# Local attention, a dense expert layer and a soft expert layer on one core: token groups of six tiles as the outermost loop, with later attention placed between the experts

## The chip, the core and the metric

The kernel runs on one core of one Trainium2 chip. Its time is the device time of one execution, in microseconds (us); lower is better. TensorE (PE, with its weight loads as PEld), VectorE (DVE), ScalarE (ACT), GpSimd (POOL) and SyncE (SP) each work through a queue of their own in a fixed order and wait for one another by semaphores. SP's work here is only to issue transfers.

## What is computed

```python
# 4 batches, 8 heads, 576 positions, head size 64; 2304 tokens of 512 values
scores = q @ k.T / sqrt(64) - slope[head] * |i - j|     # kept where 0 <= i - j < 128
x = softmax(scores) @ v                                  # tokens x 512
p = domain_probs / domain_probs.sum(-1)
x = sum over e of p[:, e] * (relu(x @ w1[e]) @ w2[e])    # 4 experts, 512 -> 1024 -> 512, every token
logits = x @ phi                                         # 32 slots, 4 for each of 8 experts
slots = softmax over tokens(logits).T @ x
slots[expert] = relu(slots[expert] @ m1[expert]) @ m2[expert]
out = softmax over slots(logits) @ slots
```

## The kernel before

There are 18 token tiles of 128 tokens. Nearly every product is made in fp16 with each operand split into a high and a low half, so that one product is three matmuls (high x high, high x low, low x high). Each split is one ACT copy and one DVE or POOL subtraction.

**Attention** runs in 72 steps, one for each tile and pair of heads, written in the loop over `n` from line 521. A step makes scores (`qk`, L364 and L369), masks and exponentiates them (L380 on DVE, L385 on ACT), splits them (L390, L391) and has them transposed by a DMA transpose that SP issues (L327, tile `eT`); three steps later the product with V follows (L411). For each tile SP also issues three loads (L304) and transposes of q, k and the result (`qT`, `kT`, `xT`). So SP issues about seven transposes a tile.

**Expert 0 of the dense layer** is laid into the attention steps: a list `pend` of pieces (L206 is the first layer, L234 the second) is worked off with a budget of about 2.8 us of matmuls a step. Tiles 0 and 1 are made in float32 (L273, L283).

**Experts 1 and 2 and half of 3** come after the attention, in units of one quarter of an expert's hidden width by six tiles (`unit_l1`, `unit_l2`). A unit's first layer replaces eight block products by seven (a Strassen-Winograd scheme with sums of x blocks, made once a group in `xsum_jobs`, L598 and L602, and sums of weight blocks, made once a quarter in `w7_jobs`, L641 and L646). It is 42 matmuls of 384 columns (L657); its second layer is 36 matmuls of 512 columns (L732). The units go expert quarter outermost, then the three groups of six tiles, so each weight quarter is loaded, split and summed once and serves three units. `l2_add` (L244) adds each unit's second layer to the accumulator in SBUF, six additions a unit.

**The other half of expert 3** is made in the plain form (L206, L234), with the soft layer's steps (`x2_tile`, `x2_log`, `x2_l`, `x2_d`) between its pieces. At last the soft layer's experts (`hp`, L1063; `so_ps`, L1081) read 64 weight blocks of 512 KB, which `pre` loads ahead (L826) into as many buffers as are free; a used buffer is filled again by `refill`. Then the outputs are made (L1094).

The order in which instructions stand on each engine is not that of the code: a scheduler decides it when the program is built, so the change can move instructions far.

Of the kernel before, what the change touches and what calls it, by code (L numbers as in the profile page):

```python
# [20 lines left out]
def kernel(  # L21
# [38 lines left out]
    slab = ctx.enter_context(tc.tile_pool(name="slab", bufs=23))  # L60
# [13 lines left out]
    def sl12(shape, dt, name):  # L74
        return slab.tile(shape, dt, tag="x12", name=nm(name), bufs=3)
# [65 lines left out]
    W = {}  # L141
    stg = {}

    def load_w(e, qd, part="ab"):
        if "a" in part:
            t = stg[e, qd, 0] = sl([P, KC, 256], F32, "stg")
            if e == 0:
# [7 lines left out]
        if "b" in part:  # L155
            t = stg[e, qd, 1] = sl([P, 2, 512], F32, "stg")
            if e == 0:
# [4 lines left out]

    def split_w(e, qd, j):
        m = j // 2
        if j % 2 == 0:
            W[e, qd, m] = sl([P, 2, 1024], F16, "w")
        a, b = (j % 2) * 512, (j % 2 + 1) * 512
        src, dst = stg[e, qd, m].rearrange("p k f -> p (k f)"), W[e, qd, m]
        nc.scalar.activation(out=dst[:, 0, a:b], in_=src[:, a:b], func=AF.Copy, scale=WS)
        nc.vector.scalar_tensor_tensor(out=dst[:, 1, a:b], in0=src[:, a:b], scalar=WS,  # L170
                                       in1=dst[:, 0, a:b], op0=ALU.mult, op1=ALU.subtract)
# [29 lines left out]
    def l1_piece(e, t0, n, fc, key):  # L201
# [7 lines left out]
        if e == 0:  # L209
            kk = (key, fc // 4)  # L210
            if kk not in hh:
                hh[kk] = sl([P, 4, 2, 256], F16, "h")
            ht = hh[kk][:, fc % 4, :, 0:n]
        else:
            kk = (key, fc // 2)
            if kk not in hh:
                hh[kk] = h3[h3n[0] % 2].rearrange("p (a b c) -> p a b c", a=2, b=2)
                h3n[0] += 1
            ht = hh[kk][:, fc % 2, :, 0:n]
# [5 lines left out]
    h3n = [0]  # L225

    def l2_mm(e, t, o, fcs, key, lo, hi):
# [3 lines left out]
        for fc in fcs[lo:hi]:  # L231
            ht = hh[key, fc // 4][:, fc % 4] if e == 0 else hh[key, fc // 2][:, fc % 2]
# [31 lines left out]
    def moe32_pieces(t):  # L264
        def l1(f0):
            if f0 == 0:
                h32[t] = sl([P, FC, P], F32, "h32")
# [31 lines left out]
    def ld(i, which="qkv"):  # L299
        for nme in which:  # L300
            src = {"q": q, "k": k, "v": v}[nme]
            t = at([P, H, D], F32, nme + "r")
# [69 lines left out]
    def soft(i, hp, st):  # L372
# [20 lines left out]
        eTt = at([P, 8, P], F16, "eT", 6)  # L393
# [4 lines left out]
    def pv(i, hp):  # L398
        if hp % 2 == 0:
            xps[i, hp // 2] = ps1.tile([P, 512], F32, tag=f"X{hp // 2}", name=nm("x"))[:, 0:4 * (D + 1)].rearrange(  # L400
# [76 lines left out]
    for qd in range(4):  # L477
        load_w(0, qd, part="b")
# [652 lines left out]
```

## Time and profile before

| | |
|---|---|
| median of 3 runs | 933.04 us (932.43 to 934.72) |
| profiled execution: span from first to last instruction | 933.0 us |
| mean granted TensorE clock | 0.984 |
| busy: PE, DVE, ACT, POOL | 878.7, 567.9, 362.0, 176.2 us |
| moved by DMA | 102.35 MB |

The profiled execution's own time is its span, 933.0 us, and the median of the runs is the same within 0.1 us, so a sum made against the span is made against the runs too. A matmul's record reaches past the point where the next one starts, so a PE shown as busy may still be slowed; the pace at which equal matmuls follow one another is the better measure of its work. Times below count from the first instruction.

### The profile page before, as it was taken

The page shows a single profiled execution, that of the slowest core. Times are in us where ns is not written, and L with a number is a line of the kernel's source. Part 1 is how long each engine was busy: PE and PEld are TensorE (multiplying, and loading weights), DVE is VectorE, ACT ScalarE, POOL GpSimd, SP SyncE. Part 2 cuts the span into 40 slices and gives each one's busy share as a digit, 9 for nine tenths or more (in the row PEclk, how much of TensorE's full clock was granted, in tenths as well). Part 3 has the DMA queues.
Part 4 walks back from the last instruction along what each step waited for, and adds up shares of the span by engine and source line. Part 5 has one row for each costly group of instructions (what it writes and reads, how often), then busy time and mean ns, then how long its engine had stood idle before and what let it go on. Part 6 is the DMA issues. An engine that isn't in the chain of part 4 may idle for free.

```text
span 933.0 us, 16170 instructions
## 1 busy us (share of the span) xinstructions
PE 878.7 (94%) x6426; PEld 517.2 (55%) x6426; DVE 567.9 (61%) x1271; ACT 362.0 (39%) x768; POOL 176.2 (19%) x173
## 2 busy tenths in 40 slices
PE   5897888898999999999999999999999999999797
PEld 4675665677675655555555555555555445564532
DVE  6775664654545997656575666666666554556612
ACT  5876665564652344323132323232333201223412
POOL 4565564554440000000000000000000005310000
PEclk9999999999999999999999999999999999999799
DMA  9889999997855110000101010101001008983796
GB/s 262 170 151 178 194 190 180 176 163 123 136 92 125 46 46 24 23 23 23 46 1 46 1 46 1 46 14 32 23 23 46 1 0 304 227 214 127 246 392 230
DMA packets 222028, 102.35 MB, mean 110 GB/s; under 512 B 187216, under 2 KB 201584, under 8 KB 221952
## 3 DMA queue, kind: packets, MB, share of 16 engines
q1 hardware_dynamic: 212320, 78.14, 39.4%
q10 hardware_dynamic: 6800, 13.11, 4.1%
q0 software_dynamic: 2832, 10.07, 3.0%
q8 instruction: 50, 0.82, 0.4%
q14 instruction: 26, 0.21, 0.1%
HBM read 64.59 MB, written 4.72 MB: 74 GB/s over the span
## 4 chain that ended last, share of the span: by engine, by line
PE 59%; issue 3%; DVE 2%; DMA 2%; POOL 1%; SPq 1%; ACT 0%; DVEq 0%; POOLq 0%; ACTq 0%
PE l L732 22%; PE A L657 12%; PE C L657 6%; PE l L206 4%; PE l L234 4%; PE B L657 3%; PE hp L1063 2%; PE so_ps L1081 2%; DMA m<-in_moe_w_dram 1%; PE fp L1094 1%; SPq L883 1%; DVE st L598 1%; POOL m L826 1%; PE lpb L892 0%; DMA xtc<-xsc 0%
## 5 line engine op out<-in xcount | busy, mean ns | idle before, releaser
L732 PE MATMUL l<-w,h 128*128 128x512 f16 x1080 | 252.8, 379 | 0.0
L244 DVE SCALAR_TENSOR_TENSOR acc<-l,pr,acc 128x512 f32<-128x512 f32 x216 | 161.6, 750 | 128.2 <-PE l L732 105.0
L657 PEld LDWEIGHTS <-w 128*128 128x128 f16 x1260 | 123.2, 98 | 95.3 <-issue 1.4
L732 PEld LDWEIGHTS <-h 128*128 128x128 f16 x1080 | 105.7, 98 | 115.2
L206 PE MATMUL l<-xT,w 128*128 128x256 f16 (+2 forms) x1152 | 150.5, 283 | 15.8 <-DVE h L221 10.9
L234 PE MATMUL l<-w,h 128*128 128x512 f16 x600 | 143.0, 379 | 0.7 <-DVE acc L244 0.7
L206 PEld LDWEIGHTS <-w 128*128 128x128 f16 x1152 | 105.9, 100 | 51.3 <-issue 17.4
L681 ACT ACTIVATE ct<-A 128x384 f32<-128x384 f32 x90 | 43.4, 487 | 205.5 <-PE A L657 205.5
L826 POOL DMA_DIRECT2D m<-in_moe_w_dram x19 | 13.7, 722 | 487.9 <-DVE h L677 424.5
L391 POOL TENSOR_TENSOR e<-e,e 128x512 f16<-128x512 f32 (+1 forms) x72 | 81.2, 1131 | 90.5 <-ACT e L390 60.8
L234 PEld LDWEIGHTS <-h 128*128 128x128 f16 x600 | 56.4, 98 | 56.7 <-issue 1.9
L220 ACT ACTIVATE h<-l 128x256 f16<-128x256 f32 (+2 forms) x96 | 36.4, 385 | 110.5 <-PE l L206 75.1
L385 ACT ACTIVATE e<-e,nmx 128x256 f32<-128x256 f32 (+1 forms) x144 | 63.4, 485 | 34.9 <-DVE nmx L380 34.7
L221 DVE SCALAR_TENSOR_TENSOR h<-l,h 128x256 f16<-128x256 f32 (+2 forms) x96 | 41.0, 432 | 54.7 <-ACT h L220 54.4
L657 PE MATMUL C<-xs,w 128*128 128x384 f16 x360 | 71.9, 326 | 0.0
L657 PE MATMUL A<-xs,w 128*128 128x384 f16 x360 | 69.6, 326 | 0.0
L657 PE MATMUL A<-xT,w 128*128 128x384 f16 x360 | 67.3, 326 | 1.0 <-issue 1.0
L380 DVE CUSTOM_DVE_ANT_0 e<-s,bias 128x256 f32<-128x256 f32 (+1 forms) x144 | 52.6, 404 | 14.4 <-PE s L369 12.7
L676 ACT ACTIVATE h<-ct 128x384 f16<-128x384 f32 x90 | 43.8, 515 | 44.6 <-PE l L732 29.2
L411 PE MATMUL x<-vv,eT 128*128 128x65 f16 (+1 forms) x816 | 42.9, 196 | 11.7 <-DMA eT<-e 9.2
L411 PEld LDWEIGHTS <-eT 128*128 128x128 f16 x816 | 36.6, 100 | 21.4 <-DMA eT<-e 12.2
L677 DVE SCALAR_TENSOR_TENSOR h<-ct,h 128x384 f16<-128x384 f32 x90 | 47.6, 553 | 1.2 <-ACT h L676 1.2
(185 smaller groups left out, 984.9 us busy)
## 6 DMA issues: line engine op xcount, KB each, us to landing
m<-in_moe_w_dram ACTq DMA_DIRECT2D x25, 512.0 KB, 6.0
stg<-in_moe_w_dram SPq DMA_DIRECT2D x20, 512.0 KB, 4.8
m<-in_moe_w_dram SPq DMA_DIRECT2D x20, 512.0 KB, 10.0
m<-in_moe_w_dram POOLq DMA_DIRECT2D x19, 512.0 KB, 12.5
stg<-in_moe_w_dram SPq DMA_DIRECT2D x24, 256.0 KB, 3.2
out_dram<-ots SPq DMA_DIRECT2D x18, 256.0 KB, 3.1
qr<-in_q_dram SPq DMA_DIRECT2D x16, 256.0 KB, 3.8
kr<-in_k_dram SPq DMA_DIRECT2D x16, 256.0 KB, 4.0
```

The source lines that it names most:

```text
L206: nc.tensor.matmul(pt, lhsT=w1_ap(e, fc, wa, kc), rhs=x_ap(t0, n, xa, kc), start=first_mm, stop=(kc == KC - 1 and wa == 1))
L234: nc.tensor.matmul(pt, lhsT=ht[:, ha, o:o + P], rhs=w2_ap(e, fc, wa), start=(fc == fcs[0] and ha == 0 and wa == 0), stop=(fc == fcs[-1] an ...
L244: nc.vector.scalar_tensor_tensor(out=a, in0=pt, scalar=p, in1=a, op0=ALU.mult, op1=ALU.add)
L380: mx = nc.vector.tensor_tensor_reduce(out=et[:, hl, c0:], in0=st[:, hl, c0:], in1=bias[:, h, c0:], op0=ALU.add, op1=ALU.min, scale=-0.125, ...
L385: nc.scalar.activation(out=et[:, hl, c0:], in_=et[:, hl, c0:], func=AF.Exp, scale=-1.0, bias=nmx[i][:, h:h + 1])
L391: nc.gpsimd.tensor_tensor(out=e2[:, :, 1], in0=et[:, :, c0:], in1=e2[:, :, 0], op=ALU.subtract)
L411: nc.tensor.matmul(o[:, 0:w], lhsT=t[:, (hl * 2 + ea) * nk + kb - kb0], rhs=vvs[i - 1 + kb][:, h, va, 0:w], start=(kb == kb0 and ea == 0 a ...
L657: nc.tensor.matmul(o, lhsT=wq_[:, blk, wa, kc], rhs=xf(xa, kc), start=(first and kc == 0 and wa == 0 and xa == 0), stop=(kc == 1 and wa == 1),
L676: nc.scalar.activation(out=o[:, 0], in_=src, func=AF.Relu)
L677: nc.vector.scalar_tensor_tensor(out=o[:, 1], in0=src, scalar=0.0, in1=o[:, 0], op0=ALU.max, op1=ALU.subtract)
L681: nc.scalar.activation(out=dst, in_=src, func=AF.Copy)
L732: nc.tensor.matmul(pt, lhsT=u["h"][:, z, ha, par, i * P:(i + 1) * P], rhs=w2_ap(e, 2 * qd + z, wa), start=(z == 0 and ha == 0 and wa == 0) ...
```

## The change

**Loops.** Token groups of six tiles (`sg`) become the outermost loop: `QU` lists 44 units, first group 0 with experts 1, 2, 3, then group 1 with 1, 2, 3, 0, then group 2 with 0 to 3. Only group 0 with expert 0 stays in the plain form, in the attention steps of the opening (`groups0` ends at tile 5). All else is made of seven products.

**Attention.** The opening runs only until group 0's expert 0 has been queued, about step 30. The other steps are spread over the units of groups 0 and 1 by `steps_to`, with goals `S_A` and `S_B`.

**Weights.** A quarter's split and summed operands are made once (`fresh`) and stored in DRAM (`keep`, 0.92 MB and 0.52 MB); 28 later units read them back (`again`), all on SP's queue.

**Second layer.** `half_l2` sums two quarters in PSUM before one addition, so three additions a unit on average instead of six.

**Buffers.** `slab` goes from 23 to 13 buffers; weights, sums and h tiles have pools of their own; the sums of x have one buffer instead of three; the matmul accumulators `A` and `B` of a unit share the two `L1` banks and `C` has one bank; raw q, k and v share four buffers, `eT` has five instead of six.

**Soft layer.** `x2_tile` and its followers of tiles 0 to 11 stand in the units of group 2. Of the 64 weight blocks 36 are loaded ahead (15 issued by POOL, the rest by SP) and 28 by `refill`; before it was 44 and 20, issued by POOL, ACT and SP.

```diff
-    slab = ctx.enter_context(tc.tile_pool(name="slab", bufs=23))
+    slab = ctx.enter_context(tc.tile_pool(name="slab", bufs=13))
+    sub = ctx.enter_context(tc.tile_pool(name="sums", bufs=1))
+    dram = ctx.enter_context(tc.tile_pool(name="dram", bufs=1, space=bass.MemoryType.DRAM))
...
+    def s12(shape, dt, name):
+        return sub.tile(shape, dt, tag="S12", name=nm(name), bufs=1)
+    def w7b(shape, dt, name):
+        return sub.tile(shape, dt, tag="w7", name=nm(name), bufs=2)
+    def h6(shape, dt, name):
+        return sub.tile(shape, dt, tag="h6", name=nm(name), bufs=5)
...
-        eTt = at([P, 8, P], F16, "eT", 6)
+        eTt = at([P, 8, P], F16, "eT", 5)
...
-    for z in [1, 1, 1, 1, 2, 2, 2, 2, 2, 2, 2]:
...
+    groups0 = [[0], [1], [2], [3], [4, 5]]
...
+    while avail:
+        n = nstep[0]
+        nstep[0] += 1
+        att_step(n, lambda: front(n))
+    def steps_to(n):
+        while nstep[0] <= min(n, NLAST):
+            att_step(nstep[0])
+            nstep[0] += 1
...
+    def keep(key, t, shape):
+        d = dW[key] = dram.tile(shape, F16, name=nm("dw"))
+        nc.sync.dma_start(out=d, in_=t)
...
+        def again():
+            W7[e, qd] = w7b(S7, F16, "w7")
+            nc.sync.dma_start(out=W7[e, qd], in_=dW["a", e, qd])
...
         def p1():
-            u["A"] = ps.tile([P, 512], F32, tag=f"S{n % 2}", name=nm("A"), bufs=1)[:, 0:N]
+            u["A"] = ps.tile([P, 512], F32, tag="L1", name=nm("A"))[:, 0:N]
...
-            u["C"] = ps1.tile([P, 512], F32, tag=f"X{n % 2}", name=nm("C"))[:, 0:N]
+            u["C"] = ps1.tile([P, 512], F32, tag="X1", name=nm("C"))[:, 0:N]
...
+    def half_l2(e, qds, sg, us, init, order):
...
+                                     start=(y == 0 and z == 0 and ha == 0 and wa == 0),
+                                     stop=(y == 1 and z == 1 and ha == 1))
+            if y == 1:
+                l2_add(e, t, l2p.pop((e, qds[0], t)), init)
...
+    QU = [(0, e, qd) for e in (1, 2, 3) for qd in range(4)]
+    QU += [(1, e, qd) for e in (1, 2, 3, 0) for qd in range(4)]
+    QU += [(2, e, qd) for e in range(4) for qd in range(4)]
...
+    def unit_jobs(x):
+        return (raw_at(x + 1, "b") + raw_at(x + 2, "a") + w2_jobs(*QU[x][1:], fresh[x]) + w7_at(x + 1))
...
+    S_A = [nstep[0] + (4 * 2 * TS + 4 - nstep[0]) * (x + 1) / 10.5 for x in range(12)]
+    S_B = [S_A[-1] + (NLAST + 1 - S_A[-1]) * (x + 1) / 14.0 for x in range(16)]
...
-    slb = ctx.enter_context(tc.tile_pool(name="slb", bufs=17))
+    slb = ctx.enter_context(tc.tile_pool(name="slb", bufs=14, reuse_waits="tile"))
...
-    pre(17, "slb")
+    pre(8, "slb")
+    pre(1, "x12")
+    for x in range(28, NU):
...
+        unit(x, sj)
+    dq[0] = nc.sync
+    pre(1, "x12")
+    pre(1, "S12")
+    pre(2, "w7")
```

**How the order changes: DVE, around attention steps 33 to 36.** Before, DVE's queue there holds attention (L380 is the masked score, L420 to L422 the normalization) and the low half of the plain first layer (L221).

```order
274 L420 TENSOR_SCALAR r_2116<-x_2028 128x4
275 L421 RECIPROCAL r_2116<-r_2116 128x4
276 L422 TENSOR_TENSOR x_2115<-x_2028,r_2116 128x256
277 L221 SCALAR_TENSOR_TENSOR h_1841<-l_307_1874,h_1841 128x256
278 L380 ISA e_2159,nmx_2050<-s_2150,bias_90 128x256
```

Now the sums of group 0's x blocks (L618 and L622, which were L598 and L602; `st` and `xs` are their tiles) stand among the scores of the following group (L392, which was L380).

```order
287 L618 TENSOR_TENSOR st_1923<-st_1923,st_1922 128x768
288 L618 TENSOR_TENSOR st_1922<-st_1922 128x768
289 L433 RECIPROCAL r_2291<-r_2291 128x4
290 L434 TENSOR_TENSOR x_1806<-x_1890,r_2137 128x256
291 L622 TENSOR_TENSOR xs_1921<-st_1923,xs_1921 128x768
292 L234 SCALAR_TENSOR_TENSOR h_1842<-l_303_1875,h_1842 128x256
293 L392 ISA e_2564,nmx_2563<-s_2558,bias_95 128x128
```

Before, no sum of x blocks and no split of summed weights (L646) stood ahead of the last score. Now group 0's sums and the first weight quarters' share DVE with attention steps 28 to 46, which the scheduler has drawn forward into the end of the opening and the first two units.

**How the order changes: SP, in the middle of the attention.** Before, SP's queue holds only transposes and loads of q, k and v.

```order
76 L327 DMA_TRANSPOSE eT_1739<-e_281_1736 128x8x128
77 L327 DMA_TRANSPOSE xT_652<-xs_1741 128x8x128
78 L327 DMA_TRANSPOSE kT_1923<-ks_1824 128x8x128
79 L304 DMA vr_2169<-in_v_dram 128x8x64
80 L327 DMA_TRANSPOSE eT_1777<-e_288_1774 128x8x128
```

Now the stores of weight operands (L655, `dw` is the DRAM tile) and their readings back (L665 and L689) stand among them, here in the first units of group 1.

```order
180 L339 DMA_TRANSPOSE eT_3905<-e_613_3902 128x8x128
181 L689 DMA w_4946<-dw_2618 128x2048
182 L655 DMA dw_4150<-w_640_4081 128x3584
183 L316 DMA raw_4675<-in_q_dram 128x8x64
184 L339 DMA_TRANSPOSE eT_4045<-e_635_4042 128x8x128
185 L339 DMA_TRANSPOSE qT_4338<-qs_4234 128x8x128
```

A store's condition is that its operand is made, a reading's that its buffer is free, and the transposes behind them now come after these in the queue.

## Rows read from the trace of the kernel before

**Rows 1.** The page, busy time of each engine.
```profile
PE 878.7 (94%) x6426; PEld 517.2 (55%) x6426; DVE 567.9 (61%) x1271; ACT 362.0 (39%) x768; POOL 176.2 (19%) x173
```

**Rows 2.** Windows: length, busy us of each engine (instructions), granted clock, DMA share, GB/s.
```profile
0.00:105.00 105.00, 82.14 (x940) 64.35 (x941) 70.69 (x239) 71.67 (x157) 58.48 (x63) 0.98 0.97 191
105.00:173.00 68.00, 57.89 (x627) 42.91 (x625) 37.99 (x140) 41.95 (x96) 35.32 (x32) 0.95 1.08 185
173.00:325.00 152.00, 143.12 (x1373) 101.67 (x1371) 92.20 (x254) 76.09 (x160) 54.86 (x47) 0.98 0.67 121
325.00:800.00 475.00, 475.00 (x2529) 247.37 (x2528) 305.95 (x516) 134.45 (x279) 18.19 (x23) 1.00 0.13 44
```

**Rows 3.** Chain of waits: start us, us, what.
```profile
311.16 1.31 PE l L206 x12
...
402.16 2.59 PE l L732 x12
...
411.24 1.95 PE A L657 x12
```

**Rows 4.** Waits of PE: us in total, times, longest.
```profile
PE l L206 <- DVE h L221: 10.9, 8, 3.3
PE x L411 <- DMA eT<-e: 9.2, 11, 1.9
```

**Rows 5.** Timeline of PE, first score products of attention steps 28 and 46.
```profile
105.19 0.22 PE L364 MATMUL s<-kT,qT 128*128 128x128 f16 x1
...
172.81 0.22 PE L364 MATMUL s<-kT,qT 128*128 128x128 f16 x1
```

**Rows 6.** Groups of DVE instructions by form: busy us, mean ns of one.
```profile
L244 DVE SCALAR_TENSOR_TENSOR acc<-l,pr,acc 128x512 f32<-128x512 f32 x216 | 161.6, 750 | 128.2 <-PE l L732 105.0 <-PE l L234 22.7
L677 DVE SCALAR_TENSOR_TENSOR h<-ct,h 128x384 f16<-128x384 f32 x90 | 47.6, 553 | 1.2 <-ACT h L676 1.2
L170 DVE SCALAR_TENSOR_TENSOR w<-stg,w 128x512 f16<-128x512 f32 x44 | 32.5, 773 | 4.0 <-ACT w L169 4.0
L221 DVE SCALAR_TENSOR_TENSOR h<-l,h 128x256 f16<-128x256 f32 x68 | 28.6, 422 | 39.8 <-ACT h L220 39.6
L646 DVE SCALAR_TENSOR_TENSOR w<-wt,w 128x1024 f16<-128x1024 f32 x10 | 12.2, 1222 | 1.1 <-ACT w L645 1.1
L602 DVE TENSOR_TENSOR xs<-st,xs 128x768 f16<-128x768 f32 x12 | 11.5, 963 | 0.9 <-ACT xs L601 0.9
L641 DVE TENSOR_TENSOR wt<-stg,wt 128x256 f32<-128x256 f32 x20 | 8.4, 422 | 0.0
L646 DVE SCALAR_TENSOR_TENSOR w<-stg,w 128x512 f16<-128x512 f32 x10 | 6.9, 691 | 0.3
L646 DVE SCALAR_TENSOR_TENSOR w<-stg,w 128x256 f16<-128x256 f32 x10 | 4.2, 424 | 0.0
```

**Rows 7.** Chain of waits, three sums in a row on DVE.
```profile
295.08 2.71 DVE st L598 x3
```

**Rows 8.** Window in which the sums are made.
```profile
300.00:350.00 50.00, 48.76 (x297) 28.77 (x295) 49.09 (x78) 23.53 (x46) 0.00 (x0) 1.00 0.16 50
```

**Rows 9.** Line L327: time SP takes to issue one (min, median, max).
```profile
L327 SPq DMA_TRANSPOSE eT<-e x64: 1207/1269/3636, 45.2 to 280.8; - x64
```

**Rows 10.** Waits of SP's queue: us in total, times, longest.
```profile
SPq L327 <- POOL e L391: 62.5, 43, 5.8
```

**Rows 11.** Chain of waits: the soft layer's experts.
```profile
881.70 7.44 PE hp L1063 x64
...
907.55 7.16 PE so_ps L1081 x64
```

**Rows 12.** Tile m: loads issued by SP, first and last start.
```profile
L826 SPq DMA_DIRECT2D m<-in_moe_w_dram x20: 368/544/1705, 880.9 to 902.6; - x20
```

**Rows 13.** Window inside these loads.
```profile
896.00:900.00 4.00, 4.00 (x44) 1.34 (x40) 0.29 (x1) 0.32 (x2) 0.00 (x0) 1.00 1.05 406
```

More of the change, by code (lines that the diff above doesn't have):

```diff
@@ L141, with load_w @@
     W = {}
+    W2 = {}
+    W7 = {}
     stg = {}
[L144 to L147, printed above, removed]
+    def load_w(e, qd, part, t=None):
+        m = "ab".index(part)
+        plain = t is not None
+        if t is None:
+            t = sl([P, 1024], F32, "stg")
+        t = stg[e, qd, m] = t.rearrange("p (k f) -> p k f", k=(KC, 2)[m])
+        if part == "a":
+            if plain:
                 src = w1[e, :, qd * 256:(qd + 1) * 256].rearrange("(k p) f -> p k f", p=P)
@@ L519, with att_step @@
     wq = [(0, qd, j) for a in (0, 2) for qd in range(4) for j in (a, a + 1)]
-    budget = 0.0
-    for n in range(NS + LAG + 3):
+    def att_step(n, work=None):
         i, hp = divmod(n, 4)
@@ L559, with front @@
                 (build_small2 if n == 9 else build_small3)()
-        for _ in range(1 if n >= 4 else 0):
-            if wq:
-                split_w(*wq.pop(0))
+        if work:
+            work()
+        for m in range(NS):
+            if pvt(m) == n:
+                pv(m // 4, m % 4)
+    budget = [0.0]
+    def front(n):
+        if n >= 4 and wq:
+            split_w(*wq.pop(0))
         while avail and avail[0][0] <= n:
@@ new lines, in f, with w7_at @@
+            if y == 1:
+                l2_add(e, t, l2p.pop((e, qds[0], t)), init)
+        return [lambda t=t, y=y: f(t, y) for t in order for y in range(2)]
+    QU = [(0, e, qd) for e in (1, 2, 3) for qd in range(4)]
+    QU += [(1, e, qd) for e in (1, 2, 3, 0) for qd in range(4)]
+    QU += [(2, e, qd) for e in range(4) for qd in range(4)]
+    NU = len(QU)
+    seen = set()
+    fresh = []
+    for sg, e, qd in QU:
+        fresh.append((e, qd) not in seen)
+        seen.add((e, qd))
+    def w7_at(x):
+        return w7_jobs(*QU[x][1:], fresh[x]) if x < NU else []
@@ L790 @@
+    for x in range(28):
+        unit(x, [])
     hh.clear()
-    sums_pool.__exit__(None, None, None)
-    slb = ctx.enter_context(tc.tile_pool(name="slb", bufs=17))
+    att.__exit__(None, None, None)
+    mp = ctx.enter_context(tc.tile_pool(name="mp", bufs=1, reuse_waits="tile"))
+    mp2 = ctx.enter_context(tc.tile_pool(name="mp2", bufs=2, reuse_waits="tile"))
+    slb = ctx.enter_context(tc.tile_pool(name="slb", bufs=14, reuse_waits="tile"))
     m2q = []
@@ L1033 @@
     sip = ps.tile([P, KC, NSL], F32, tag="S0", name="sip", bufs=1)
-    cT.extend([h.rearrange("p (a t) -> p a t", a=2) for h in h3] + [mp.tile([P, 2, 2 * P], F16, name="cT1")])
+    cT.append(mp.tile([P, 2, 2 * P], F16, name="cT1"))
     x2_d(NG - 1)
-    pre(8)
+    pre(2)
     dq[0] = nc.sync
```

362 lines of the change are left out of this document (190 added, 172 removed).

## The prediction

> **What bounds the kernel now.** I read the busy times first. PE is busy 94% of the span, DVE 61% [rows 1], so PE is the bound; but a matmul's record overlaps the next, so I went on to windows and pace. In the 475 us from 325 to 800 PE is never idle and its granted clock is 1.00 [rows 2]. There matmuls follow one another at their pace: twelve of 512 columns in 2.59 us, 0.216 each, twelve of 384 in 1.95, twelve of 256 in 1.31 [rows 3]. That is 2.37 columns a nanosecond in all three, so that stretch can only shrink by columns left out.
>
> The losses lie elsewhere. From 0 to 105 us PE is idle 22.9 us, from 105 to 173 10.1 us, from 173 to 325 8.9 us, and in these the granted clock averages 0.98, 0.95 and 0.98, where the long stretch has 1.00 [rows 2]; the missing 0.05 of 68 us is 3.4 us, the missing 0.02 of 152 us 3.0. So the second half of the attention, 173 to 325, costs 8.9 + 3.0 = 11.9 us beside PE's own work. The causes are many small waits, such as 10.9 us for the low half of h on DVE and 9.2 us for a transposed `eT` [rows 4]. SP works hard there: a transpose takes 1.2 to 1.3 us to issue [rows 9], seven a tile, and what it waits for most is POOL's split, 62.5 us [rows 10].
>
> **The change in PE's columns.** The order gives the matmul columns of the whole program: 1,933,280 before and 1,901,024 after. The 32,256 fewer are 14 quarter units of six tiles whose first layer goes from 72 x 256 = 18,432 columns to 42 x 384 = 16,128. At 0.216 us for 512 columns that is 13.6 us less, all of it on the path wherever PE is the bound.
>
> I divide the program by two marks: the first score of attention step 28 and that of step 46, at 105.2 and 172.8 us in the trace [rows 5]. By the order the columns before, between and behind the marks were 110,768, 121,472 and 1,701,040; they become 116,400, 119,392 and 1,665,232. In time at full pace: 46.7, 51.2 and 717.6 us become 49.1, 50.4 and 702.5.
>
> **The opening, to step 28.** Loads, first scores and float32 tiles are the same, and 2.4 us of PE work have moved into it. I add these 2.4 whole. Raw q, k and v in four buffers and `eT` in five instead of six could delay it; each load still has the buffer of something used a step before, so I take nothing. The bounds are 0 (the work falls into idle time) and 8 us.
>
> **Steps 28 to 46.** Before they took 67.6 us for 51.2 us of PE work. After, PE has 50.4 us, but DVE gets more. What DVE did there was 38.0 us busy [rows 2]. Ten splits of the plain first layer go away (18 to 8), 10 x 0.42 = 4.2 us. Added are, by the order and the forms of [rows 6]: 8 sums of x and 4 splits of them, 12 x 0.96 = 11.5; 8 splits of second-layer weights, 6.2; 16 weight sums, 6.7; three quarters' summed weights, 3 x (1.22 + 0.69 + 0.42) = 7.0; 9 splits of h and 8 additions of products in units 0 to 2, 17 x 0.55 = 9.4; two additions to the accumulator, 1.5. Together 42.3. Back to back they overlap a little: three sums took 2.71 us where 3 x 0.96 is 2.88 [rows 7], some 0.09 for each of 61, 5.3 us. So DVE needs 38.0 - 4.2 + 42.3 - 5.3 = 70.8 us, more than PE. DVE can be kept full: while the sums were made before, it was busy 49.1 of 50 us and PE was still idle only 1.2 [rows 8]. 70.8 / 0.98 is 72 us, and I take 72, 4.4 more than before. The bounds are 62 (if the overlap of its attention instructions is also greater when they crowd) and 85 (if the waits that left DVE idle 30.0 of 68 us return in part). SP is no tighter here: 18 steps are 4.5 tiles, 32 transposes at 1.3 us, 42 us, and some 60 loads and stores, which I price by the smallest issue of a load in [rows 12], 0.37, to its median, 0.54: 22 to 32 us, 64 to 74 in all, of which the last few stand behind the mark.
>
> **After step 46.** PE's work falls by 15.1 us. The 11.9 us of attention loss fall away as such, since the remaining 26 steps are spread over units of 42 x 0.1625 + 36 x 0.216 = 14.6 us, about one and a half steps a unit, with ready matmuls between them. I keep half of the idle 8.9 us, 4.5. Each change of group has to make new sums in a single buffer while PE waits for the first summed product; [rows 8], where two sets of sums were made at a loss of 1.2 us, gives 1.2 each, 2.4. That makes 7 us, a gain of 4.9. DVE, halved in its additions to the accumulator (0.75 us each), has slack here: it was busy 306 of 475 us before [rows 2].
>
> The two shared `L1` banks, the single `C` bank, stores and most readings back I cost at nothing; their cover is the other unit's second layer. At the end of an even quarter, two second-layer pieces and one first-layer block, 1.3 + 1.0 + 1.3 us, lie between the last product in `A` and the next unit's use of that bank, against one split of 0.55 us on DVE. Without that cover each of 44 units would lose up to 1 us.
>
> **The end.** The soft layer's experts run from 881.7 to 907.6 + 7.2 = 914.7 [rows 11]. Their loads come at 406 GB/s [rows 13], 1.29 us for a block of 512 KB, and SP needs only about 0.54 us to issue one [rows 12], so the transfers bind, not the issue. Before, 20 refills were due in this stretch; now 28 are. The first can go when the first quarter of the first products is done, 1.9 us in; 28 x 1.29 = 36.1, so the last lands at 881.7 + 1.9 + 36.1 = 919.7, and with half a microsecond of matmuls that is 5.5 us later than before. I take 6, with bounds of 2 and 20. The Trainium skill (DMA: Bandwidth & Descriptors, Where 436 GB/s comes from) puts the memory side's limit for one core at about 358 GB/s; this trace's 406 is above it. By 358 a block would take 1.46 us, the end would be 10 us later instead of 5.5, and the sum some 4 us higher; the row decides.
>
> **The sum.** 933.0 + 2.4 (opening) + 4.4 (steps 28 to 46) - 15.1 (columns) - 4.9 (attention spread) + 6 (end) = 925.8; I predict 926 us. The span stands for the median, which it equals.
>
> **The rivals.**
>
> *Well packed, 910 us.* DVE needs only 64 us for steps 28 to 46 because crowded instructions overlap more, the spread steps lose 3 us instead of 7, and refills cost 2. Then 933.0 + 2.4 - 3.6 - 15.1 - 8.9 + 2 gives 910. For it speaks that PE lost 1.2 us in [rows 8] with DVE full; against it, 10 us idle in the same steps before.
>
> *SP's queue holds attention back, 938 to 950 us.* One queue now carries transposes, loads, stores and readings. A reading of summed weights must wait for one of two buffers, which is free only when the unit before the last is through, and transposes behind it wait too. PE then stands at a product with V that it meets in its fixed order. Group 1 has 12 such readings of 0.92 MB; if each holds PE for its own transfer at 406 GB/s, 2.3 us, it costs 27 us; for half of that, 13. That is 938 to 953. From 7 us (933 - 926), 0.6 us a reading, it decides the sign. For it speaks that SP is busy or waiting through the attention [rows 9, 10]; against it, that a step now has some 9 us instead of 67.6 / 18 = 3.8. The Trainium skill (DMA: Bandwidth & Descriptors, Anatomy of one DMA) says that DMA engines wait for no semaphore and that each wait is on the issuing sequencer before dispatch; by that rule a waiting reading does hold all behind it, and the trace agrees as far as the 62.5 us of waits are SP's own.
>
> *Late blocks at the end, 937 us.* 21 of the 36 early loads are SP's, and stand near or behind the last unit. If ten of them are still under way when the experts start, 10 x 1.29 = 13 us come on top, less the 2 us that overlap.
>
> *Nothing gained, 932 us.* DVE's queue, with splits waiting for ACT between sums, takes 78 us for steps 28 to 46. The other terms hold, and the saving is eaten.
>
> **How the numbers follow.** Forecast 0.45 (mostly 919 to 931), well packed 0.20, SP's queue 0.17, late blocks 0.08, nothing gained 0.10. The range that leaves out two in ten goes from the price of the well-packed case to the middle of SP's: 910 to 945. A difference under 0.3%, 2.8 us, can't be told from none. Faster (under 930.2): 0.20 and 0.38 of the forecast, 0.58. Same: 0.07 of the forecast and the last case, 0.17. Slower: 0.25.
>
> **What would show it.** Right: the first score of step 28 near 107 us and of step 46 near 180; between them DVE busy over 90% and PE idle more than the 10.1 us of before; from there to the last unit PE at its pace, idle under 10 us, clock 1.00; `so_ps` ending 38 to 40 us after the first `hp`, against 33. Wrong: step 46 at 165 or 195, PE waiting for `eT` or `qT` in group 1 by more than 15 us with SP waiting at a reading, or blocks of `m` that land after the experts could use them by more than 10 us. I would be wrong most easily in DVE's 72 us, which has the widest bounds.

## The result, and the profile after

The changed kernel is slower: 942.51 us (median of nine runs, 939.59 to 944.87) against 934.46 for the kernel before in the same session (nine runs, 930.79 to 939.21), a ratio of 1.0082 with a 95% interval of 1.0058 to 1.0107. I had forecast 926. The profiled execution took 939.59 us with a span of 937.7, so it lies at the low end of its runs, and some 3 us of the distance to the median stand in no trace here. Two of the eight runs of `c_qp` below, 949.15 and 949.48, were slow ones, over 1.5% above its fastest, and are left out of its time.

The page's busy times (answering [rows 1]) have hardly moved, though 32,256 columns are gone. Its PE line, and then the windows of [rows 2], with one for the stretch from step 28 to step 46 (columns as there):

```profile
PE 877.4 (94%) x6150; PEld 492.2 (52%) x6150; DVE 572.4 (61%) x1247; ACT 399.8 (43%) x816; POOL 182.6 (19%) x169
```

```profile
0.00:105.00 105.00, 80.77 (x841) 62.42 (x842) 68.49 (x213) 68.89 (x148) 53.27 (x60) 0.93 0.87 179
105.00:173.00 68.00, 54.93 (x555) 38.26 (x552) 58.63 (x156) 44.47 (x97) 37.65 (x30) 0.90 1.09 211
173.00:325.00 152.00, 145.27 (x978) 80.37 (x976) 127.24 (x269) 84.73 (x167) 30.35 (x22) 1.00 0.89 235
325.00:800.00 475.00, 471.25 (x2940) 253.46 (x2939) 266.01 (x511) 167.30 (x339) 61.37 (x58) 1.00 0.50 145
114.20:188.30 74.10, 59.01 (x529) 39.05 (x527) 65.87 (x165) 51.42 (x110) 36.34 (x28) 0.91 1.12 231
```

The loss is at the front: in the first 173 us PE is idle 37.3 us (24.2 and 13.1), before 33.0, and the granted clock fell from 0.98 and 0.95 to 0.93 and 0.90. PE's timeline at the two marks of the prediction (answering [rows 5], which had 105.19 and 172.81):

```profile
114.22 0.22 PE L376 MATMUL s<-kT,qT 128*128 128x128 f16 x1
...
188.30 0.22 PE L376 MATMUL s<-kT,qT 128*128 128x128 f16 x1 [0.76 <-DVE nmx L392]
```

Step 28 came at 114.2 us (forecast 107), step 46 at 188.3 (forecast 180), 74.1 us apart (forecast 72).

To compare kernels whose steps lie in other places I use one measure throughout: PE's **loss** up to a mark is the time passed less the time that all matmuls issued by then take at their pace (for each form the lower quartile of the distances from one start to the next). Worked out from each trace:

```
loss of PE, us, up to    50     75    125    225    400    600    850    end | matmuls at pace
before                  24.5   29.1   41.6   58.8   63.9   64.1   67.4  109.1 | 818.0
after                   30.4   36.9   47.6   68.5   73.6   74.6   81.8  129.3 | 803.3
o_ord                   27.6   32.8   43.9   57.7   64.9   65.8   73.0  120.0 | 804.0
c_psum                  27.2   33.8   45.8   58.6   67.5   69.1   77.0  124.5 | 802.3
f_early                 25.0   41.3   49.1   70.0   79.5   80.5   87.7  134.9 | 803.7
x_pin0                  31.1   39.0   48.0   63.6   66.9   67.5   75.0  122.9 | 803.3
x_pin                   28.0   34.5   46.4   55.4   59.4   60.6   68.1  115.8 | 803.1
x_best                  27.2   32.4   45.2   53.8   57.5   59.1   66.0  111.2 | 804.0
```

The end is that of the last matmul. Below, `o_ord` has the opening's loads in the former order, `c_psum` in addition group 0's sums on POOL, `f_early` a piece of tile 0 earlier; `x_pin0` and `x_pin` hold the later attention steps in place, without and with `o_ord`'s edit; `x_best` is the best of all.

So the columns gave 14.7 us, and 20.2 were lost: 9.7 by 225 us and 0.8 more by 600; 3.9 more between 600 and 850, in the soft layer's steps; 5.8 at the end.

Each line is one execution, and the early marks vary from one to the next. `e_8` below has the same order of instructions on PE, DVE, ACT and POOL as the changed kernel, and has lost 3.0 us more by 225; `s_sp`, in `o_ord`'s order on PE up to 626 us, 3.3 more. From 225 to 600 either pair agrees within 0.6. So a difference of 3 us by 225 says nothing without the times beside it.

### The profile page after: what moved, and what is told of

The parts are those of the page before. It is cut to its first block, busy times and chain, and to the rows that moved or that the text cites. A ratio compares the mean times of both kernels' runs of the same rounds, so it can differ in the third digit from the quotient of the medians.

```text
span 937.7 us, 15861 instructions
## 1 busy us (share of the span) xinstructions
PE 877.4 (94%) x6150; PEld 492.2 (52%) x6150; DVE 572.4 (61%) x1247; ACT 399.8 (43%) x816; POOL 182.6 (19%) x169
## 4 chain that ended last, share of the span: by engine, by line
PE 73%; DMA 11%; DVE 8%; ACT 2%; issue 2%; POOL 1%; SPq 0%; DVEq 0%; POOLq 0%; ACTq 0%
PE l L778 32%; PE A L703 16%; PE C L703 8%; PE B L703 4%; DMA m<-in_moe_w_dram 3%; DMA qT<-qs 3%; DMA eT<-e 2%; PE x L423 2%; PE l2f L295 2%; DVE w L184 1%; PE l L226 1%; PE fp L1197 1%; PE l L246 1%; DMA xtb<-xsb 1%; DVE st L618 1%
## 5 line engine op out<-in xcount | busy, mean ns | idle before, releaser
L703 PEld LDWEIGHTS <-w 128*128 128x128 f16 x1848 | 176.4, 98 | 135.0 <-issue 8.3
L256 DVE SCALAR_TENSOR_TENSOR acc<-l,pr,acc 128x512 f32<-128x512 f32 x120 | 89.3, 746 | 49.0 <-PE l L778 48.4
L726 ACT ACTIVATE ct<-A 128x384 f32<-128x384 f32 x132 | 63.2, 485 | 114.2 <-PE A L703 111.4
L703 PE MATMUL A<-xT,w 128*128 128x384 f16 x528 | 100.5, 326 | 4.4 <-DVE ct L730 3.0
L721 DVE SCALAR_TENSOR_TENSOR h<-ct,h 128x384 f16<-128x384 f32 x132 | 83.2, 631 | 35.1 <-ACT h L720 35.1
L703 PE MATMUL A<-xs,w 128*128 128x384 f16 x528 | 101.0, 326 | 1.1 <-ACT ct L726 0.7
L703 PE MATMUL C<-xs,w 128*128 128x384 f16 x528 | 101.8, 326 | 0.0
L730 DVE TENSOR_TENSOR ct<-ct,C 128x384 f32<-128x384 f32 x88 | 48.1, 546 | 38.7 <-ACT ct L726 34.9
L392 DVE CUSTOM_DVE_ANT_0 e<-s,bias 128x256 f32<-128x256 f32 (+1 forms) x144 | 52.6, 402 | 15.1 <-PE s L381 12.0
L376 PE MATMUL s<-kT,qT 128*128 128x128 f16 x272 | 44.1, 230 | 10.8 <-DVE nmx L392 7.4
L703 PE MATMUL B<-xT,w 128*128 128x384 f16 x264 | 50.3, 326 | 0.7 <-DVE h L721 0.7
L402 ACT ACTIVATE e<-e 128x512 f16<-128x512 f32 (+1 forms) x72 | 42.9, 598 | 13.0 <-DMA eT<-e 12.3
```

The costliest lines, as they stand in the source:

```text
L256: nc.vector.scalar_tensor_tensor(out=a, in0=pt, scalar=p, in1=a, op0=ALU.mult, op1=ALU.add)
L376: nc.tensor.matmul(o, lhsT=qT[i][:, 0, h], rhs=mv, start=True, stop=False)
L392: mx = nc.vector.tensor_tensor_reduce(out=et[:, hl, c0:], in0=st[:, hl, c0:], in1=bias[:, h, c0:], op0=ALU.add, op1=ALU.min, scale=-0.125, ...
L703: nc.tensor.matmul(o, lhsT=wq_[:, blk, wa, kc], rhs=xf(xa, kc), start=(first and kc == 0 and wa == 0 and xa == 0), stop=(kc == 1 and wa == 1),
L721: nc.vector.scalar_tensor_tensor(out=o[:, 1], in0=src, scalar=0.0, in1=o[:, 0], op0=ALU.max, op1=ALU.subtract)
L726: nc.scalar.activation(out=t, in_=u["A"], func=AF.Copy)
```

## Experiments

Each edit is of the changed kernel unless a run is named as its base. Ratios are to the kernel before on the same chip; its median went from 933.07 to 934.86 between sessions, so differences between runs below are those of the ratios, times 934 us.

**Two edits of the loads, and what they have in common.** `o_ord` issues the opening's loads in the former order, `o_raw` gives raw q, k and v six buffers again.

```diff
-            ld(1, "q")
-    ld(1, "k")
+            ld(1, "qk")
+    ld(1, "v")
     for qd in range(4):
         load_w(0, qd, "b", arena.pop(0))
-    ld(1, "v")
```

> The changed kernel with the loads of the opening issued in the order of the kernel before: q and k of tile 1 between the second and third quarter of expert 0's first-layer weights, v of tile 1 ahead of the second-layer weights. Theory 'load order': the opening's extra loss (first score of step 28 at 114.2 us, where 107.5 was forecast) comes from this order; then step 28 starts at 106 to 108 and the time falls by 6 to 8 us, to about 935. Rival 'raw buffers': the loss comes from the four shared buffers of raw q, k and v, which hold the loads of tiles 3 and up back (v of tile 3 was issued at 35.3 us, before at 26.9); then this run changes step 28 by less than 2 us. Rival 'order of the rest': the order of DVE's and PE's queues in the opening is only chosen otherwise by the scheduler; then any change may move step 28 by some us either way, and v of tile 3 stays late.

```diff
-            t = at([P, H, D], F32, "raw", 4)
+            t = at([P, H, D], F32, nme + "r")
-    slab = ctx.enter_context(tc.tile_pool(name="slab", bufs=13))
+    slab = ctx.enter_context(tc.tile_pool(name="slab", bufs=12))
```

> The changed kernel with two buffers each for raw q, k and v as in the kernel before (six in place of four); to make room, slab has 12 buffers in place of 13. Theory 'raw buffers': v of tile 3 is issued near 27 us again, step 28 starts at 106 to 109, and the time falls by 5 to 8 us, unless the lost slab buffer costs later. Rival 'load order': step 28 stays at 113 to 115. If the slab buffer is missed, the loss stands in the units (weights read back later) or in fewer early blocks of m, some 1.3 us each at the end, not ahead of step 28.

`o_ord` took 933.34 us, ratio 0.9989 (0.9971 to 1.0006): 8.7 us back. But not by its theory: on SP only one load of the opening moved, v of tile 1, by one place, and v of tile 3 was issued at 37.2 us, later still. Step 28 came at 111.3, so 2.9 of the 9.0 us are back at that mark, and the rest of the gain lies behind it. What changed is the order on the other engines, which the scheduler made anew (PE's differs from 27.8 us on, DVE's from 23.9). `o_raw` took 938.38 (1.0041, 1.0017 to 1.0064); its loss by 225 us was 59.8, with v of tile 3 at 28.5; it lost 7.5 us later, at 550 (last section). So two different edits give 10.8 and 8.7 us of loss back by 225, the one without more buffers, the other without the former load order: neither the buffers nor the load order makes the loss by itself. The two together stay a rival here; `f_best0` below bears on it.

**Is it luck of the order?** One small piece of DVE work placed a step later, in both kernels, and the new load order in the kernel before.

```diff
-        if n in (9, 24):
+        if n in (10, 24):
             with tc.issue_after(mx):
-                (build_small2 if n == 9 else build_small3)()
+                (build_small2 if n == 10 else build_small3)()
```

> The changed kernel with one small piece of work placed one attention step later (the six DVE instructions on the domain probabilities and phi: step 10 in place of 9); the scheduler then orders the rest of the opening otherwise too (1548 lines of PE's order differ). Theory 'luck of the order': the 9.2 us that the load order gave back are not the loads' (on SP only v of tile 1 moved, by one place), but the order's, which any edit of the opening changes; then this run lands anywhere from 931 to 945, and more likely below 942.5 than not, with the clock of the first 115 us between 0.93 and 0.99 as its sign. Rival 'a real cost of the change': the shared buffers or the loads hold the opening back; then this run stays within 2 us of 942.5.

> The kernel before with the same small piece of work one attention step later. Theory 'luck of the order': the kernel before has an order of its own, whose opening can be had better or worse; its time moves by some us from 934.5, as likely up as down. Rival 'a real cost of the change': the opening of the kernel before is not sensitive, and this stays within 1.5 us of 934.5.

> The kernel before with the opening's loads in the changed kernel's order (k of tile 1 behind the first-layer weights of expert 0, v of tile 1 behind the second-layer weights). Theory 'load order': it costs here what it cost there, 6 to 9 us, and the time is 941 to 944. Theory 'luck of the order': it moves by some us either way, and no more likely up than down. Rival 'only with shared buffers': the kernel before has six buffers for raw q, k and v, and stays within 1.5 us.

`n_small` 940.35 (1.0059, 1.0040 to 1.0077), `b_small` 932.04 (0.9975, 0.9959 to 0.9991), `b_ord` 933.59 (0.9972, 0.9952 to 0.9991). Three orders of the changed kernel spread over 8.7 us (1.0082, 1.0059, 0.9989), three of the kernel before over 2.6. The new load order costs the kernel before, with its six buffers, nothing; "load order" by itself falls. The changed kernel's own order is a poor one among these three, and its time moved more with the order. Three orders are few, and `n_small` is a weak neighbour: its order on PE is the changed kernel's up to 79 us, so it leaves what happens before that as it was, and the 8.7 us are `o_ord`'s alone.

**Is DVE's queue the bound of steps 28 to 46?** Group 0's sums go to POOL, in the changed kernel's order (`p_sum`) and in `o_ord`'s (`c_psum`).

```diff
-            nc.vector.tensor_tensor(out=o, in0=x, in1=y, op=op)
+            (nc.gpsimd if sg == 0 else nc.vector).tensor_tensor(out=o, in0=x, in1=y, op=op)
...
-            nc.vector.tensor_tensor(out=XU[sg][:, b, 1], ...
+            (nc.gpsimd if sg == 0 else nc.vector).tensor_tensor(out=XU[sg][:, b, 1], ...
```

> The changed kernel with the eight sums and the four low halves of group 0's x blocks made by POOL instead of DVE; the later groups' stay on DVE. Theory 'DVE's queue': steps 28 to 46 took 74.1 us because DVE was full; 11.5 us leave it, so the stretch takes 62 to 66 us and the time falls by 6 to 11 us. Rival 'chains of waits': the stretch is bound by splits and transposes that wait in turn, and POOL, which makes the low half of e and of x there, is slower a piece; then step 46 moves by less than 3 us or comes later, and waits for POOL appear ahead of the transposes.

> The changed kernel with the load order of the run o_ord and with group 0's sums of x on POOL. In o_ord DVE was busy 81.2 of the 85 us from 115 to 200, where the changed kernel had 76.5. Theory 'DVE's queue' in its narrower form: DVE binds this stretch only once the opening's order leaves it no pauses; then taking 11.5 us from it gives 4 to 9 us against o_ord, 924 to 929. Rival 'chains of waits': the stretch stays as long because each step waits for split, transpose and scores in turn, and the time stays within 2 us of o_ord's 933.3 or rises.

941.03 us (1.0074, 1.0055 to 1.0093) and 933.45 (0.9994, 0.9974 to 1.0015): 0.7 us gained in the one and 0.5 lost in the other, less than the intervals can tell from nothing. The same window in `o_ord` and in `c_psum`:

```profile
115.00:150.00 35.00, 27.11 (x255) 19.48 (x254) 33.52 (x69) 22.28 (x45) 21.24 (x15) 0.90 1.14 201
```

```profile
115.00:150.00 35.00, 26.55 (x228) 18.59 (x227) 23.17 (x52) 19.35 (x40) 30.89 (x22) 0.85 1.05 196
```

DVE lost 10 of its 33.5 busy us there and PE got nothing of it (27.1, then 26.6). But the two windows do not hold the same work. PE's first score of step 46 in `o_ord`, then in `c_psum` and `p_sum`:

```profile
193.30 0.22 PE L376 MATMUL s<-kT,qT 128*128 128x128 f16 x1
```

```profile
265.98 0.22 PE L376 MATMUL s<-kT,qT 128*128 128x128 f16 x1
```

```profile
246.70 0.22 PE L376 MATMUL s<-kT,qT 128*128 128x128 f16 x1
```

The scheduler made these orders anew too, and moved later steps far back: between 115 and 150 us `o_ord` starts seven steps (31 to 37), `c_psum` four (30 to 33). POOL, which got the sums, is busy 30.9 of the 35 us. What is shown is that the forecast gains, 6 to 11 and 4 to 9 us, did not come. That DVE's queue does not bind the crowded steps is not shown, since the test changed the steps and filled POOL.

**SP's queue.** On the base of `o_ord`, stores and readings back go to POOL's queue (`c_qp`, three `nc.sync` to `nc.gpsimd`), or the loads of raw weights do (`c_raw`, two).

> The run o_ord with the stores of weight operands and their readings back issued on POOL's queue instead of SP's. Theory 'SP's queue holds attention back': transposes no longer stand behind stores and readings, and the time falls by 4 us or more, most of it between 170 and 225 and in group 1. Rival 'readings are hidden': in group 1 PE lost only 1 to 2 us outside the change of group, so at most 2 us come back; POOL, which issues each in about 0.7 us and waits for the operand in its fixed order, may lose as much.

> The run o_ord with the loads of raw weights (all but those of the opening) issued on POOL's queue instead of SP's. Theory 'bursts of loads': between 157 and 163 us SP issued seven such loads in a row, with transposes behind them, and an eT took 6.6 and a qT 7.8 us at such a place in the changed kernel; moved, 2 to 5 us come back between 150 and 225. Rival 'transfers collide': the DMA share there is 1.1 and more, the transposes are slow because the engines are full, whichever queue issues; then it stays within 2 us, or rises, since POOL makes e's low half there.

`c_qp` 939.65 (1.0070, 1.0038 to 1.0103; its runs spread from 934.9 to 945.8, and the profiled one is the fastest, so its trace does not show the loss), `c_raw` 949.75 (1.0176, 1.0141 to 1.0210). Neither gains: in `c_qp` the loss by 400 us is 66.4, in `o_ord` 64.9, and in `c_raw` POOL's fixed order puts step 28 at 123.5. PE's longest waits in the changed kernel from the last crowded step to the end of group 1's attention (188 to 500 us) say the same:

```profile
PE A L703 <- DVE ct L730: 3.0, 1, 3.0
PE l L778 <- DVE acc L256: 1.3, 2, 1.0
PE A L703 <- DVE w L679: 1.1, 2, 0.8
```

No transposed tile is among them, though SP itself waited 11.0 us at a reading. In the crowded steps, 114 to 190 us, PE waits 5.6 us for `eT`; there SP waits most for POOL's low half of e (9.8 us), at a store never over 0.7. The rival whose time came true (938 to 953) was not what happened.

**The end.** `e_8` leaves out the last eight loads of weight blocks; the products of these eight read the block loaded last before them.

```diff
+    cut = m2q[-8:]
+    del m2q[-8:]
+    same = {c: m2q[-1] for c in cut}
```

> The changed kernel without the last eight loads of weight blocks of the soft layer's experts: these eight blocks' products use the block loaded last before them, so that part of the computation has other data; 20 refills are left, as many as in the kernel before. Theory 'refills bind the end': from the first hp to the end of so_ps 40.7 us become about 33, and the time falls by 6 to 8 us. Rival 'late early loads': the end waits for the early loads that SP issues near the last unit, which stay; then it falls by less than 3 us.

935.70 us (1.0013, 0.9999 to 1.0027): 6.4 less than the changed kernel. Start and end of the experts on PE, in the changed kernel and in `e_8` (the matmuls of `so_ps` overlap the last ones; before, [rows 11]):

```profile
878.61 8.38 PE L1166 MATMUL hp<-m,siT 128*32 128x512 f32 x64
...
915.20 1.05 PE L1184 MATMUL so_ps<-m,hT 128*32 128x512 f32 x4 [0.30 <-DMA m<-in_moe_w_dram]
916.57 1.05 PE L1184 MATMUL so_ps<-m,hT 128*32 128x512 f32 x4 [0.31 <-DMA m<-in_moe_w_dram]
...
919.13 1.05 PE L1184 MATMUL so_ps<-m,hT 128*32 128x512 f32 x4 [0.21 <-DMA m<-in_moe_w_dram]
```

```profile
881.75 8.73 PE L1172 MATMUL hp<-m,siT 128*32 128x512 f32 x64
...
909.92 7.07 PE L1190 MATMUL so_ps<-m,hT 128*32 128x512 f32 x64
```

With all 28 refills the last products come in pairs (two records a matmul), each pair waiting for its block, 1.37 us apart; without eight of them the last ones run in one piece. From the first `hp` to the end of `so_ps` it is 41.6 us, and 35.2 without the eight, 0.8 for each.

**The strips of the soft layer's sum.** On the base of `o_ord`, priority for four float32 matmuls.

```diff
+        with tc.high_priority():
             for j in range(4):
                 nc.tensor.matmul(sp[32 * j:32 * j + 32], lhsT=dd[:, j], ...
```

> The run o_ord with one edit: the four float32 matmuls of a soft group's sum (sp, one for each strip of 32 columns) are given priority, so that group 0's stand together in PE's order; in o_ord other matmuls stand between them. Theory 'strips apart': side by side the four take 0.99 us, apart 0.97 us each, so three of them, 2.9 us, come back and the time is 930 to 931; in the windows from 625 to 665 PE's loss against its pace falls from 3.2 and 1.1 us to about 1.2 in all. Rival 'hidden': the time stays at 933 because PE is not the end of that stretch.

929.88 us (0.9969, 0.9947 to 0.9990): 1.9 us below `o_ord` by the ratios, whose intervals overlap; 2.9 were expected. The chain of waits of the changed kernel, then of `s_sp` (two records a matmul):

```profile
635.45 0.97 PE sp L1052 x2
...
642.05 0.98 PE sp L1052 x2
...
644.11 0.98 PE sp L1052 x2
...
658.81 0.97 PE sp L1052 x2
...
698.20 0.99 PE sp L1052 x8
```

```profile
629.38 0.99 PE sp L1052 x8
```

Four matmuls into four strips of 32 rows take 0.99 us side by side and 0.97 each when others stand between them. The trace is clearer than the times: from 600 to 850 the loss falls from 7.2 to 4.1.

**Steps spread as the code says.** `x_pin` (on `o_ord`) queues each later step's scores on PE behind the unit's last matmul ahead of it; `x_pin0` does it in the changed kernel's own order, `x_pin1` in that of `n_small`.

```diff
-                nc.tensor.matmul(o, lhsT=wq_[:, blk, wa, kc], ...)
+                last[0] = nc.tensor.matmul(o, lhsT=wq_[:, blk, wa, kc], ...).ins
...
+        if n < NS and last:
+            with tc.issue_after(last[0]):
+                st = qk(i, hp)
```

> The run o_ord with the scores of each later attention step queued on PE behind the last matmul of the unit's piece ahead of it in the code, so that steps 30 to 46 are spread over units 0 to 7 instead of being drawn ahead of and into units 0 to 2. Theory 'drawn ahead': PE loses its time from 125 to 225 us because 16 steps are crowded there with the work of the first weights, each step waiting for its own splits and transposes; spread, each has some 7 us, and PE's loss from 125 to 225 falls from 13.8 to below 8, the time to 926 to 929. Rival 'DVE's queue': the DVE work of the first units alone fills that time; then less than 2 us come back. Rival 'nothing to fill': the units' first weights come too late (their buffers are free only at the end of expert 0), and PE waits without the steps; then the time rises.

> The changed kernel in its own load order, with nothing but the scores of the later attention steps queued behind the unit's last matmul ahead of them, as in x_pin. Theory 'drawn ahead' as the whole cause: the time comes down to x_pin's, 925 to 929, since the opening's other order costs only through the steps it crowds into 125 to 200 us. Theory 'two causes': the opening's order has its own price, and this lands 4 to 9 us above x_pin, 930 to 935. Rival 'the pin needs the other order': it stays above 937.

> The run x_pin0 with the small piece of work one attention step later, as in n_small. Theory 'drawn ahead': the unit part is now fixed by the code, so this and x_pin0 differ by less than 3 us, where the changed kernel and its reorderings spread over 9. Theory 'two causes': they may differ by as much as before, through the opening alone.

`x_pin` 926.24 (0.9933, 0.9909 to 0.9956), `x_pin0` 931.32 (0.9976, 0.9956 to 0.9995), `x_pin1` 932.25 (0.9985, 0.9966 to 1.0005). In its own order the changed kernel gains 9.9 us by this alone, in `n_small`'s 6.9, and these two orders now lie 0.8 apart, where they lay 2.1. `x_pin` from 115 to 150, against the row of `o_ord` above, then `x_pin0`:

```profile
115.00:150.00 35.00, 30.35 (x262) 20.88 (x263) 28.59 (x54) 17.65 (x35) 12.53 (x8) 0.90 0.89 186
```

```profile
115.00:150.00 35.00, 25.55 (x235) 17.64 (x233) 27.25 (x59) 17.70 (x35) 12.69 (x10) 0.80 0.90 169
```

PE does 30.4 us there in place of 27.1, in `x_pin0` only 25.6; its gain comes behind 150 us. From 125 to 225 the loss is 9.0 in `x_pin`, 15.6 in `x_pin0`, 13.8 in `o_ord` and 20.9 in the changed kernel. From 225 to 400, with the change from group 0 to group 1, 4.0 are lost in `x_pin`, 7.2 in `o_ord`. That spreading the steps gains is shown by the times, in three orders; by which wait is not. DVE too has less to do in `x_pin`'s window (28.6 us, 33.5 in `o_ord`), and `c_psum`, whose steps 34 to 46 lie at 158 to 266 us (165 to 264 in `x_pin`), gained nothing: either the first of the steps drawn forward cost, or POOL's added work ate the gain. That `x_pin0` stays 4.0 us above `x_pin`, with intervals that just touch, says that the opening's order has a price of its own.

**What in the opening's order costs it?** One reading of the traces: the float32 second layer of tile 0 (`l2f`) stands ready behind scores that wait. By the order it follows step 9 in the kernel before, 12 in `o_ord`, 13 in the changed kernel. Windows and PE's timeline of the changed kernel, then of `o_ord`:

```profile
43.00:50.00 7.00, 2.15 (x34) 1.72 (x31) 6.18 (x20) 5.34 (x12) 5.07 (x5) 0.89 1.03 199
50.00:60.00 10.00, 10.00 (x26) 4.42 (x24) 2.47 (x7) 4.70 (x9) 3.60 (x3) 0.74 1.11 208
```

```profile
46.49 0.23 PE L376 MATMUL s<-kT,qT 128*128 128x128 f16 x1 [2.57 <-DMA qT<-qs]
...
49.95 9.75 PE L295 MATMUL l2f<-stg,h 128*128 128x512 f32 x16
```

```profile
43.00:50.00 7.00, 5.97 (x53) 4.50 (x51) 6.35 (x30) 6.03 (x14) 4.34 (x4) 0.85 1.01 196
50.00:60.00 10.00, 7.52 (x73) 4.51 (x71) 6.65 (x18) 7.24 (x15) 5.03 (x5) 1.00 1.22 213
```

```profile
47.49 7.11 PE L295 MATMUL l2f<-stg,h 128*128 128x512 f32 x16
```

PE is idle for 4.9 of 7 us, and then the same 16 records take 9.75 us instead of 7.11, at a mean clock of 0.74, that is with part of them at the lower of the two levels, 1.2 instead of 2.4 GHz. `f_early` puts `l2f` behind step 8, `f_best` does so in `x_best` (next). In both, tile 0's result is scaled by domain probabilities that are not yet normalized, since the piece now comes ahead of that in the code.

```diff
         late[:] = l2
+        if tl[0] == 0:
+            pend.extend(l2)
+            late.clear()
```

> The changed kernel in its own load order with one edit: the float32 second layer of tile 0 (l2f, 8 products) is put in the list of pieces right behind its first layer, so that it stands in PE's order behind the scores of step 8 instead of step 13 (in the kernel before it stands behind step 9, in o_ord behind step 12). Theory 'ready work behind scores that wait': the changed kernel's opening loses 43.8 to 49.9 us at scores of tile 3 that wait for qT, while l2f stands ready behind them, and then runs l2f at a granted clock of 0.74 (9.75 us instead of 7.1); moved, PE's loss up to 75 us falls from 36.9 to 30 to 33, and the time by 4 to 8 us, to 934 to 938. Rival 'the wait is only moved': steps 10 to 13 wait all the same and nothing ready is left for later; then the loss up to 125 us stays near 47.6 and the time within 2 us of 942.5.

> The run x_best (load order, spread steps, strips together) with the float32 second layer of tile 0 placed early as in f_early. Theory 'ready work behind scores': x_best already had l2f one step earlier than the changed kernel, so a smaller part comes back, 2 to 4 us: 918 to 921. Rival 'only moved': 922 to 924.

946.02 us (1.0143, 1.0118 to 1.0167) and 929.38 (0.9966, 0.9951 to 0.9981), 5.7 and 7.6 us slower than their bases. The loss at 50 us did fall, from 30.4 to 25.0, but from 50 to 75 it rose by 16.3 (6.5 in the changed kernel). The window, and PE's longest wait after 60 us:

```profile
50.00:60.00 10.00, 3.13 (x36) 2.44 (x36) 10.00 (x27) 10.00 (x22) 2.69 (x2) 0.62 0.42 84
```

```profile
PE tpf L441 <- DVE x L434: 10.1, 1, 10.1
```

Tile 1's transposes now wait 10.1 us for its normalized x, while DVE and ACT are full for ten microseconds. The wait was only moved: the rival was right. With the changed kernel's load order in place of `o_ord`'s the same version, `f_best0`, took 930.52 (0.9976, 0.9954 to 0.9999). It had been expected within 3 us of `f_best` if the load order counts only through the place of `l2f`, and 4 or more above it if it has another price. It is 0.9 above, and PE's order is now the same in 6085 of 6150 places; without this edit it was in 5339 (`x_pin` and `x_pin0`), and the times lay 4.0 apart. So where the scheduler makes nearly the same order of either, the load order costs little even with four buffers; the intervals leave room for 3 us.

**Together.** `x_best` is `x_pin` with the edit of `s_sp`.

> The run x_pin with the priority for the strips of s_sp. Both theories: the two edits lie in different stretches, so 3 us come off x_pin's 926.2: 922 to 925, a ratio near 0.990 to the kernel before.

922.45 us (0.9885, 0.9855 to 0.9915; 921.20 to 924.39): 18 us below the changed kernel and 11 below the kernel before. From 600 to 840 us it loses 4.0 us, `x_pin` 7.1, which is the strips' part; the mark at 850 lies behind the last unit of either. Its page:

```profile
PE 868.7 (94%) x6150; PEld 489.1 (53%) x6150; DVE 568.4 (62%) x1247; ACT 398.8 (43%) x816; POOL 180.9 (20%) x169
```

## Why the prediction was wrong, step by step

- **Columns** (13.6 us for the program): right. PE's matmuls at their pace take 14.7 us less.
- **The opening** (2.4 us, and "each load still has the buffer of something used a step before, so I take nothing"): this is the step that failed. It cost 9.0 us, past the upper bound of 8: the 2.4 of work came as forecast, and 6.6 of PE's loss with it. The four buffers need not be the reason: `o_ord` keeps them, moves one load by one place, and regains the loss by 225 us. At step 28 itself it regains only a part: the mark is 6.1 us later than before with 3.1 more of work ahead of it, so 3.0 of the 6.6 stay. What I left out is that the scheduler orders every engine anew, and that the time moves with this order: by 8.7 us where no load of q, k or v of tiles 0 to 4 was issued more than 1.4 us sooner (`o_ord`), and by 0.9 where the loads differ and PE's order hardly does (`f_best0`). The price of the opening's order with the later steps fixed is 4.0 us (`x_pin0` less `x_pin`). What in the order costs that stays open: the one reading that I tried, `l2f` behind waiting scores, was taken away and another wait came.
- **Steps 28 to 46** (72 us "by DVE"): the size was nearly right (74.1), which is no proof of the mechanism. DVE was busy 65.9 of the 74.1 us (89%, where I had put over 90). Moving 11.5 us of its work to POOL gave nothing, twice, but with the steps moved and POOL filled this does not settle whether DVE's queue binds. The steps drawn forward into the first units, crowded with the work on the first weights, cost the time: spread out, the kernel is 9.9 us faster in its own order, 6.9 in `n_small`'s and 5.2 in `o_ord`'s. Which of the waits in a crowded step binds, DVE's among them, I did not separate; it stays open. I had seen in the order that the steps are drawn forward and priced the stretch as a sum of one engine's work; I should have asked whether they had to stand there.
- **After step 46** (attention spread, -4.9): right. From step 46 to 600 us the loss is 9.8 us (64.8 at the mark), before 13.8 (50.3 at the mark, 64.1 at 600), 4.0 less. The group change took 3.4 us at 350 where I had 1.2, the spread steps less. PE was at a clock of 1.00.
- **The soft layer's steps**, which I did not price: 3.9 us more loss between 600 and 850, of which 2.9 are group 0's strips set apart (three extra times 0.97); `s_sp` gave back 3.1 of the loss there.
- **The end** (+6): right in size, 5.8 of loss and 6.4 us by `e_8`; the experts themselves took 41.6 us where I had 38 to 40.

In times of the profile: 925.8 forecast, plus 6.6 (opening), 2.1 (steps 28 to 46) and 3.2 (behind them) is the span of 937.7. With the edit that takes the crowding away and an order that happens to be better, the kernel takes 926.2 (`x_pin`), the forecast's time, and with the strips, which the forecast did not have, 922.5. That 926 is met so closely is in part luck, since not all of its terms were right; but a gain of that size could be had, and the order gave it back.

Of the rivals, SP's queue predicted the right time for a wrong reason, of late blocks there is no sign (in `e_8` the last products run in one piece), nothing gained had DVE as its cause, which is neither shown nor excluded, with 78 us for a stretch that took 74.1, and well packed was out of reach since the loss by 225 us rose by 9.7 instead of falling.

## What to carry to other kernels

Where a scheduler sets the order, time a change together with two or three neutral reorderings of both kernels before judging it: here one load moved by one place was worth 8.7 us, as much as the change seemed to cost. A busy engine is the bound only if taking work from it moves the end; test that before costing a stretch by its queue, and look in the order of the tested kernel whether the rest still stands where it stood: here the same edit moved attention step 46 by 58 and 73 us. Work that is meant to be spread must be tied to its place in the order of the engine that it waits on, since a scheduler that draws it forward spends the spread.

## What the runs showed of the hardware that was not expected

- A DMA transpose can hold its queue for long. Before, SP mostly needed 1.2 to 1.3 us to issue one, 3.6 at most ([rows 9]). Soon after POOL had issued seven or eight loads of 512 KB, two took 4.95 us together in the changed kernel and 19.36 in `o_raw`, the first of these 13.95 alone, and PE then waited 5.8 us. That the loads are the reason was not tried. SP's timeline in either:

```profile
554.95 4.95 SPq L977 DMA_TRANSPOSE xtb<-xsb  x2
560.00 6.99 SPq L977 DMA_TRANSPOSE xtc<-xsc  x2
```

```profile
546.28 19.36 SPq L977 DMA_TRANSPOSE xtb<-xsb  x2
```

- An idle stretch can count twice. In the changed kernel, whose first 105 us had a mean granted clock of 0.93, 4.9 us of idle within 7 were followed by matmuls that took 2.6 us longer (9.75 less 7.11), in a window with a clock of 0.74, where `o_ord` had 1.00.
